# Packing six of eight head groups of an attention block without padding, with a dense output projection for them

## Chip, cores and metric

One NeuronCore of a Trainium2 chip runs the whole program. The metric is the device time of one execution in microseconds (us), of which the median over several runs is used. The kernel before takes 896.84 us (three runs, 896.48 to 897.79).

## What is computed

The input `x` has 2048 rows of 640 columns in bf16. The reference is a transformer block of two parts, with 32 heads of 20 columns each:

```
qkv = layernorm(x) @ wqkv                      # 640 -> 3 x 32 heads x 20
p   = softmax(q @ k.T * 20 ** -0.5)            # per head, 2048 x 2048
h   = x + concat_heads(p @ v) @ wo             # output projection 640 -> 640
l   = layernorm(h)
h2  = h + ((l @ w_gate) * (l @ w_up)) @ w_down # 640 -> 1728 -> 640
```

## The kernel before

**Tiling.** A head of 20 columns is padded to a slot of 32 partitions (`SLOT`), so that four heads (`HPG`) fill the 128 partitions and make a *group*; there are eight groups (`NG`). Queries are taken in four blocks of 512 rows (`QB`, `NB`), and parts of blocks 1 to 3 in halves of 256 (`PASS`, `SPLIT_G`; the passes are named "0", "1", "E", "F", "2", "C", "D", "3", "A", "B"). One pass of one group over all 2048 keys is a *segment*.

**Main loop.** The segments are cut into score tiles of 1536 columns. For each tile the loop emits the score matmuls (`emit_S`, L557), then the exponential on ScalarE from PSUM to a bf16 tile `E` or `El` (L573). For some tiles the last 512 columns are left to VectorE, which computes the exponential with four operations of its own (`emit_x` and its steps: L610, L620, L621, L615). Then the products with the values are accumulated in `acc` (`emit_AV`, L795); an extra row of ones in the values yields the softmax sums. When a segment is complete, VectorE copies `acc` to `asb` (L807).

**Normalisation.** `norm` sends the four rows of sums through DRAM by transfers on SyncE's queue: `sums` out (L666), `sums_all` back in 128 partitions (L667), a reciprocal `ri` on VectorE (L677), `scr` out (L679), and four broadcasts `bc` (L682). A planned number of tiles later `times` multiplies `asb` by `bc` and writes the group's normalised output, a padded 128 x 512 tile `on` (L685). The last group of a half block is not sent through DRAM but normalised on TensorE (`job_norm`: L700, L708, L710, L711, L716, L731), since its result is wanted soonest; the segments so treated are listed in `FAST`. All transfers of the kernel are issued in order on one queue, SyncE's.

**Output projection.** `wo` is held as eight tiles `wo0` to `wo7` of 128 x 640, each with four heads' 20 rows at 32-row steps and zeros between (`load_wo`: eight memsets L987, 32 loads L991). Before that, the first five of these tiles stage a part of `wqkv` at the start of the kernel. `out_mm` computes 128 rows of the output in two halves of 320 columns, each a chain of eight matmuls over the groups (L1052), and VectorE adds `x` (L1056). These jobs, like those of the second layernorm and of the gated part (`glu`, L1221, L1226, L1229) and its last product (`y`, L1270, L1274), are run in pieces in the gaps that the score matmuls leave on TensorE.

**What sets the order.** A planner in the Python code keeps estimates of each engine's time (`at`), the cost of each job and of what is left (`PE_NS`, `ALONE_NS`, used in `room`), and decides from them when a piece of a job runs, when VectorE takes a share of a tile (`x_takes`), and when TensorE gets filler matmuls whose result is not used (`keep_warm`, L508; `cool`, L553). The instruction order of each engine is thus fixed when the program is built, and a changed estimate shifts all that follows.

**The end.** After the last exponential, `last_tail` handles the last 256 rows alone. `out_most` (L1376, L1378) puts `x` and seven of eight groups in PSUM for four half rows, while the last group is normalised on TensorE and VectorE (L700, L708 to L711, L716, L1391); `out_last` (L1382) adds the eighth. Then come the second layernorm (L209 onwards), the gated part (L1203, L1211) and `y`, with nothing of the attention beside them. A general path for inputs whose sums are out of range (`general`) is built as well and not run.

Of the kernel before, what the change touches and what calls it, by code (L numbers as in the profile page):

```python
# [10 lines left out]
BF16 = mybir.dt.bfloat16  # L11
# [5 lines left out]
ALU = mybir.AluOpType  # L17
AX = mybir.AxisListType

P = 128  # L20
S = 2048
D = 640
H = 32
DH = 20
# [3 lines left out]
SLOT = 32  # L28
HPG = 4
NG = H // HPG  # L30
VS = DH + 1
VW = H * VS + (SLOT - VS) + 1
QB = 512
# [5 lines left out]
HALF = D // 2  # L39
FP = 7  # L40
FPW = 256
G1 = 4
SPLIT_G = {"1": 4, "2": 2, "3": 1}
QA = 3 * QB
RES0 = 3
# [24 lines left out]
FULL_IN, FULL_NS, ALL_NS = 2083, 300, 760  # L70
X_LEAST, X_OUT, X_SOON = 2, 5, 4
X_CHUNK = 3
PE_NS = {"out": 6000, "glu": 23000, "y": 7000}
NF_NS = 1800
ALONE_NS = {"out": 4350, "glu": 15260, "y": 5710}
PART_NS, TILE_NS, ROOM = 31500, 700, 2500
E_BUFS, E_LATE = 6, 2
SHIFT = 544.0
# [13 lines left out]
def kernel(  # L92
# [11 lines left out]
    nc = tc.nc  # L104
# [7 lines left out]
    const = pool("const")  # L112
    qkp = pool("qkp")
    vp = pool("vp")
    onp = pool("onp")
# [18 lines left out]
    shift_row = const.tile([P, 1], F32, name="shift_row")  # L134
    huge = const.tile([P, 1], F32, name="huge")
    half = const.tile([P, TPB], F32, name="half")
    wo = [const.tile([P, D], BF16, name=f"wo{g}") for g in range(NG)]
    N_SUMS = 16 * (NB * NG)
    sums_all = const.tile([P, N_SUMS], F32, name="sums_all")

# [2 lines left out]
    qsp = [dram.tile([P, S], BF16, name=f"qsp{g}", bufs=1) for g in range(NG)]  # L143
    kT = [qkp.tile([P, S], BF16, name=f"kT{g}") for g in range(NG)]
    vx = [vp.tile([P, VW], BF16, name=f"vx{t}") for t in range(NT)]
    On = [onp.tile([P, QB], BF16, name=f"on{g}") for g in range(NG)]

    lnT = ra.tile([P, KT, S], BF16, name="lnT")
    wv = [ra.tile([P, D], BF16, name=f"wv{c}") for c in range(KT)]
    wqk = [ep.tile([P, EW], BF16, name="E") for c in range(KT)]  # L150
# [20 lines left out]
        nc.sync.dma_start(xs[0][:, t, :], x2d[t * P:(t + 1) * P, :])  # L171

    def wqk_half(c, hf):
        return (wo if hf else wqk)[c][:, 0:D].rearrange("p (m x) -> p m x", m=2)

    def load_wqk(hf):
        for c in range(KT):
# [170 lines left out]
    for s, (p, g, lo, hi, _) in enumerate(segs):  # L348
        w = PASS[p][2]
        n = BANK // w  # L350
# [305 lines left out]
    def read_out(b):  # L656
        return all(("om", b, t) in done for t in TAILS[b])

    def norm(s, asb):
        p, g = segs[s][0:2]  # L660
        b, c0, w = PASS[p]
        n = w // 32
        r16 = sums_all[:, col["n"]:col["n"] + n]
        col["n"] += n
        sums = dram.tile([HPG, w], F32, name="sums", tag=f"sums{w}")
        nc.sync.dma_start(sums[:], asb[DH:P:SLOT, 0:w])  # L666
        nc.sync.dma_start(r16, sums[:].rearrange("j (c f) -> (j c) f", f=n))  # L667

        due = at["dve"] + SUMS_NS

        def back():
            if at["pe"] < due and now["i"] < n_tiles:
                later(1, back)
                return
            ri = nrm.tile([P, n], F32, name="ri", tag=f"ri{n}")
            dve(130)
            nc.vector.reciprocal(ri[:], r16)  # L677
            scr = dram.tile([HPG, w], F32, name="scr", tag=f"scr{w}")
            nc.sync.dma_start(scr[:].rearrange("j (c f) -> (j c) f", f=n), ri[:])  # L679
            bc = nrm.tile([P, QB], F32, name="bc")  # L680
            for j in range(HPG):
                nc.sync.dma_start(bc[SLOT * j:SLOT * (j + 1), 0:w], scr[j:j + 1, :].to_broadcast([SLOT, w]))  # L682

            def times(asb, bc, p, g, c0, w):
                nc.vector.tensor_tensor(On[g][:, c0:c0 + w], asb[:, 0:w], bc[:, 0:w], ALU.mult)  # L685
                done.add(("n", p, g))
                yield 605 * w // QB

            def mult():
                if b and not read_out(b - 1):  # L690
                    later(1, mult)
                    return
                aux.append(times(asb, bc, p, g, c0, w))
            later(7, mult)
        later(4, back)
# [173 lines left out]
    m32, r = rstd_act(pair_mv[0], 2, lambda: bn(pair_mv[1], 0, xs[0][:, 2, :]))  # L869
# [11 lines left out]
    m32, r = rstd_act(pair_mv[1], 2)  # L881
# [101 lines left out]
                add(("v", t, 1), job_V(t, 1))  # L983

    def load_wo():
        for g in range(NG):
            nc.vector.memset(wo[g][:], 0.0)  # L987
            yield 230
            for j in range(HPG):
                h = HPG * g + j  # L990
                nc.sync.dma_start(wo[g][SLOT * j:SLOT * j + DH, :], A_wo[DH * h:DH * h + DH, :])  # L991
            due = at["pe"] + WO_NS
            while at["pe"] < due and not now["forced"]:
                yield WAIT

    def make_identf():
        nc.vector.tensor_copy(identf[:], ident[:])
# [49 lines left out]
    def out_mm(on, st, t):  # L1047
        for hf in range(2):
            ps = bank()
            cs = slice(hf * HALF, (hf + 1) * HALF)  # L1050
            for g in range(NG):
                nc.tensor.matmul(ps[:, 0:HALF], lhsT=on[g][:, t * P:(t + 1) * P], rhs=wo[g][:, cs],  # L1052
                                 start=(g == 0), stop=(g == NG - 1))
                if g == NG - 1:
                    dve(408, 136)
                    nc.vector.tensor_tensor(st["h"][t][:, cs], ps[:, 0:HALF], st["xr"][t][:, cs], ALU.add)  # L1056
                yield 136
            done.add(("oh", t, hf))
            yield NEXT
# [306 lines left out]
    def last_tail():  # L1366
        st = tail_st[LAST_B]
        on = On
        asb = final["asb"]
        c0 = LAST_T[0] * P  # L1370
        ps_h = {}

        def out_most(t, hf):
            ps = ps_h[t, hf] = bank()
            cs = slice(hf * HALF, (hf + 1) * HALF)
            nc.tensor.matmul(ps[:, 0:HALF], lhsT=ident[:], rhs=st["xr"][t][:, cs], start=True, stop=False)  # L1376
            for g in range(NG - 1):
                nc.tensor.matmul(ps[:, 0:HALF], lhsT=on[g][:, t * P:(t + 1) * P], rhs=wo[g][:, cs], start=False, stop=False)  # L1378

        def out_last(t):  # L1380
            for hf in range(2):
                nc.tensor.matmul(ps_h[t, hf][:, 0:HALF], lhsT=on[NG - 1][:, t * P:(t + 1) * P],  # L1382
                                 rhs=wo[NG - 1][:, hf * HALF:(hf + 1) * HALF], start=False, stop=True)
        ta, tb = LAST_T
        out_most(ta, 0)
        bc = sums_to_rows(sums_on_pe(asb, HW), HW)
        out_most(ta, 1)
        ps = rows_to_cols(bc, HW, accp.tile([P, QB], F32, name="acc"))
        for k in range(2):
            cs = slice(k * P, (k + 1) * P)  # L1390
            nc.vector.tensor_tensor(on[NG - 1][:, c0 + k * P:c0 + (k + 1) * P], asb[:, cs], ps[:, cs], ALU.mult)  # L1391
        out_most(tb, 0)
        out_last(ta)
        out_most(tb, 1)
        out_last(tb)
        mv = small.tile([P, 2, 2], F32, name="mv")
        for k, t in enumerate(LAST_T):
            bn(mv, k, None, [ps_h[t, hf][:, 0:HALF] for hf in range(2)])
        m32, r = rstd_act(mv, 2)
        mr = small.tile([P, 2], F32, name="mr")  # L1400
        nc.vector.scalar_tensor_tensor(mr[:], m32[:], -1.0, r[:], ALU.mult, ALU.mult)
        ls = {t: late["s"].tile([P, D], BF16, name="ln2") for t in LAST_T}
        for hf in range(2):
            cs = slice(hf * HALF, (hf + 1) * HALF)
            nc.vector.tensor_scalar(ls[ta][:, cs], ps_h[ta, hf][:, 0:HALF], m32[:, 0:1], r[:, 0:1], ALU.subtract, ALU.mult)
            nc.scalar.activation(ls[tb][:, cs], ps_h[tb, hf][:, 0:HALF], ACT.Identity, bias=mr[:, 1:2], scale=r[:, 1:2])
        begun = at["pe"]
        while at["pe"] - begun < LN_NS and step() is not None:
            pass
        idle_n = int((LN_NS - (at["pe"] - begun)) / 216)  # L1410
        if idle_n > 0:
            warm_ps = bank()
            for _ in range(idle_n):
                nc.tensor.matmul(warm_ps[:], lhsT=ident[:], rhs=kT[0][:, 0:BANK], start=True, stop=True)
        run(job_T(ls[ta], st["ln2T"][:, :, ta * P:(ta + 1) * P], "dve", mip.tile([P, D], BF16, name="mi", tag="mi")))
        run(job_T(ls[tb], st["ln2T"][:, :, tb * P:(tb + 1) * P], "act", accp.tile([P, QB], F32, name="acc")[:].bitcast(BF16)[:, 0:D]))
        fill()
        for t in LAST_T:
            for hf in range(2):
                nc.scalar.copy(st["h"][t][:, hf * HALF:(hf + 1) * HALF], ps_h[t, hf][:, 0:HALF])  # L1420
        st["w", 2] = [w_tile(src, 2, ep.tile([P, EW], BF16, name="E")) for src in (B_w_up, B_w_gate)]
        n_next = 0
        for c in job_glu(st, LAST_T, tuple(range(RES0, FP)) + tuple(range(RES0))):
            n_next += c == NEXT
            if c == NEXT and n_next == 8:
                ok = flag_ok()
            if c == NEXT and n_next == 20:
                flag_bad(ok)
        run(job_y(st, LAST_T, True))
# [85 lines left out]
    def general():  # L1515
        st = new_st(None)
        st["res"] = {}
        with tc.For_i(0, S, P) as r0:
# [3 lines left out]
            for g in range(NG):  # L1522
# [39 lines left out]
                nc.vector.tensor_tensor(oq[:, :, 0:DH], ov[:, :, 0:DH], ri[:].to_broadcast([P, HPG, DH]), ALU.mult)  # L1562
                ps = bank(BF16, P)
                nc.tensor.transpose(ps[:], oq[:].rearrange("p j e -> p (j e)"), ident[:])
                nc.vector.tensor_copy(On[g][:, 0:P], ps[:])
            for fn in (job_out(On, st, [0], None), job_glu(st, [0]), job_y(st, [0])):
                for _ in fn:
                    pass
# [33 lines left out]
```

## Time and profile before

| | |
|---|---|
| median of three runs | 896.84 us |
| the profiled execution | 900.67 us |
| its span in the profile | 898.8 us |
| ScalarE (ACT) busy | 852.7 us, 95% |
| TensorE (PE) busy | 813.7 us, 91% |
| VectorE (DVE) busy | 773.7 us, 86% |
| all transfers | 60.15 MB, a mean of 67 GB/s |

In the profile PE is TensorE's matmuls, PEld its weight loads, DVE VectorE, ACT ScalarE, POOL GpSimd, and SPq the queue of SyncE, on which the transfers are issued. A row of a timeline gives the start in us, the time to the end of the last of the instructions merged in it, the engine, the line, the operation, and `out<-in`; in brackets is the idle time of the engine ahead of it and what ended that. A row of waits gives the total in us, the number of times, and the longest. Windows give busy us and the number of instructions of each engine in a stretch, then the clock that TensorE was granted (1.00 is full), the share of the transfer engines and GB/s.

### The profile page before, as it was taken

The page shows a single profiled execution, that of the slowest core. Times are in us where ns is not written, and L with a number is a line of the kernel's source. Part 1 is how long each engine was busy: PE and PEld are TensorE (multiplying, and loading weights), DVE is VectorE, ACT ScalarE, POOL GpSimd, SP SyncE. Part 2 cuts the span into 40 slices and gives each one's busy share as a digit, 9 for nine tenths or more (in the row PEclk, how much of TensorE's full clock was granted, in tenths as well). Part 3 has the DMA queues.
Part 4 walks back from the last instruction along what each step waited for, and adds up shares of the span by engine and source line. Part 5 has one row for each costly group of instructions (what it writes and reads, how often), then busy time and mean ns, then how long its engine had stood idle before and what let it go on. Part 6 is the DMA issues. An engine that isn't in the chain of part 4 may idle for free.

```text
span 898.8 us, 21965 instructions
## 1 busy us (share of the span) xinstructions
PE 813.7 (91%) x8921; PEld 374.1 (42%) x8921; DVE 773.7 (86%) x1448; ACT 852.7 (95%) x719; POOL 31.4 (3%) x122
## 2 busy tenths in 40 slices
PE   7889999989999899889999998998899999999997
PEld 5333232222233344544444554443434455444465
DVE  7778899999999899789999998999889988889842
ACT  6999999999999999989999999999999999999951
POOL 4100000000002000001000000001000000000000
PEclk9999999999999999989999999999989999999999
DMA  6030010011034556432214334111441312010310
GB/s 198 25 65 2 1 28 25 15 36 28 14 84 112 122 146 198 112 88 66 54 51 122 81 96 107 47 30 29 121 121 45 85 31 74 15 44 9 94 38 18
DMA packets 110763, 60.15 MB, mean 67 GB/s; under 512 B 37976, under 2 KB 107652, under 8 KB 110656
## 3 DMA queue, kind: packets, MB, share of 16 engines
q1 hardware_dynamic: 110656, 58.68, 25.0%
q8 instruction: 72, 1.18, 0.6%
q14 instruction: 35, 0.29, 0.1%
HBM read 48.09 MB, written 7.28 MB: 62 GB/s over the span
## 4 chain that ended last, share of the span: by engine, by line
ACT 56%; PE 21%; issue 13%; DVE 9%; DMA 1%; SPq 0%; ACTq 0%; DVEq 0%
ACT E L573 46%; ACT El L573 10%; PE sc L557 5%; PE mi L1221 3%; PE acc L795 3%; PE f L1203 2%; PE mi L306 1%; PE mi L1052 1%; DVE xv L610 1%; PE mi L1270 1%; PE f L1270 1%; DVE xt L620 1%; DVE xt L621 1%; DVE xe L615 1%; DVE hh L1229 1%
## 5 line engine op out<-in xcount | busy, mean ns | idle before, releaser
L573 ACT ACTIVATE E<-sc 128x1536 bf16<-128x1536 f32 (+1 forms) x560 | 694.0, 1387 | 7.3 <-PE sc L557 6.0
L557 PE MATMUL sc<-qa,kT 32*128 32x256 bf16 (+1 forms) x2176 | 204.1, 320 | 23.8 <-ACT E L573 13.5
L557 PEld LDWEIGHTS <-kT 32*128 32x128 bf16 x3136 | 85.2, 92 | 223.9 <-issue 193.4
L610 DVE TENSOR_SCALAR xv<-sc 128x512 f32<-128x512 f32 x199 | 137.1, 690 | 47.3 <-PE sc L557 44.4
L573 ACT ACTIVATE El<-sc 128x1536 bf16<-128x1536 f32 (+1 forms) x123 | 159.7, 1371 | 0.6 <-PE sc L557 0.5
L795 PE MATMUL acc<-E,vx 128*32 128x256 bf16 (+1 forms) x2245 | 158.2, 315 | 0.6 <-DVE vx L271 0.6
L615 DVE SCALAR_TENSOR_TENSOR xe<-xt,xv 128x512 int16<-128x512 f32 x199 | 134.3, 681 | 0.8
L621 DVE SCALAR_TENSOR_TENSOR xt<-xt,xv 128x512 f32<-128x512 f32 x199 | 133.2, 680 | 0.6
L620 DVE SCALAR_TENSOR_TENSOR xt<-xv 128x512 f32<-128x512 uint16 x199 | 132.1, 679 | 0.3 <-DVE ri L677 0.2
L306 PE MATMUL mi<-lnT,wp 128*128 128x512 bf16 x305 | 86.5, 381 | 7.1 <-DVE qa L313 3.4
L795 PEld LDWEIGHTS <-vx 128*32 128x32 bf16 x3136 | 62.2, 96 | 62.5 <-issue 60.6
L557 PE MATMUL sc<-qb,kT 32*128 32x256 bf16 (+1 forms) x960 | 69.0, 283 | 3.4 <-ACT E L573 2.2
L1270 PE MATMUL mi<-wd,hh 128*128 128x320 bf16 x378 | 65.5, 301 | 1.1 <-DVE xr L1274 1.0
L1221 PE MATMUL mi<-ln2T,wg 128*128 128x256 bf16 x390 | 56.7, 274 | 8.6 <-DVE u L1226 7.2
L1221 PE MATMUL mi<-ln2T,wu 128*128 128x256 bf16 x390 | 55.5, 274 | 7.4 <-DVE hh L1229 7.2
L795 PE MATMUL acc<-El,vx 128*32 128x256 bf16 (+1 forms) x579 | 60.6, 294 | 0.5 <-ACT El L573 0.5
L795 PE MATMUL acc<-xe,vx 128*32 128x256 bf16 (+1 forms) x312 | 57.3, 306 | 0.0
L1270 PEld LDWEIGHTS <-hh 128*128 128x128 bf16 x448 | 37.9, 97 | 29.5 <-issue 18.2
L1221 PEld LDWEIGHTS <-wg 128*128 128x128 bf16 x390 | 33.6, 97 | 30.0 <-issue 25.3
L306 PEld LDWEIGHTS <-wp 128*128 128x128 bf16 x310 | 24.8, 97 | 50.6 <-issue 38.5
L1221 PEld LDWEIGHTS <-wu 128*128 128x128 bf16 x390 | 33.8, 97 | 28.3 <-issue 25.1
L1052 PE MATMUL mi<-wo,on 128*128 128x320 bf16 x224 | 41.6, 312 | 2.3 <-DVE xr L1056 2.2
(152 smaller groups left out, 623.0 us busy)
## 6 DMA issues: line engine op xcount, KB each, us to landing
wu<-in_B_w_up_dram SPq DMA_DIRECT2D x38, 320.0 KB
wg<-in_B_w_gate_dram SPq DMA_DIRECT2D x37, 320.0 KB
bc<-scr SPq DMA_DIRECT2D x60, 64.0 KB
bc<-scr SPq DMA_DIRECT2D x108, 32.0 KB
qsp<-qa SPq DMA_DIRECT2D x8, 384.0 KB
xr<-in_A_x_dram SPq DMA_DIRECT2D x16, 160.0 KB
out_dram<-xr SPq DMA_DIRECT2D x14, 160.0 KB
wd<-in_B_w_down_dram SPq DMA_DIRECT2D x13, 160.0 KB
```

The costliest lines, as they stand in the source:

```text
L306: nc.tensor.matmul(ps[:], lhsT=wslice(m, g, c), rhs=lnT[:, c, ch * QB:(ch + 1) * QB], start=(c == 0), stop=(c == KT - 1))
L557: nc.tensor.matmul(sc[:, o:o + w], lhsT=kT[g][SLOT * j:SLOT * (j + 1), kt * P:(kt + 1) * P], rhs=q_of(g, b, c0, w)[SLOT * j:SLOT * (j + 1) ...
L573: exps = nc.scalar.activation(e[:, 0:n_act], sc[:, 0:n_act], ACT.Exp, bias=EXP_BIAS, scale=SM_SCALE)
L610: took = nc.vector.tensor_scalar(v[:], ps, X_SCALE, X_BASE, ALU.mult, ALU.max)
L615: nc.vector.scalar_tensor_tensor(e[:], t[:], X_R, v[:], ALU.mult, ALU.add)
L620: lambda: nc.vector.scalar_tensor_tensor(t[:], u, X_P, u, ALU.add, ALU.mult),
L621: lambda: nc.vector.scalar_tensor_tensor(t[:], t[:], X_Q, u, ALU.add, ALU.mult),
L795: nc.tensor.matmul(acc["t"][SLOT * j:SLOT * (j + 1), 0:w], lhsT=vx[kt][:, VS * h:VS * h + SLOT], rhs=e, start=(acc["n"][j] == 0), stop=(ac ...
L1052: nc.tensor.matmul(ps[:, 0:HALF], lhsT=on[g][:, t * P:(t + 1) * P], rhs=wo[g][:, cs], start=(g == 0), stop=(g == NG - 1))
L1203: nc.tensor.matmul(ps[:, 0:n], lhsT=st["w", fp][k][:, c, f_cols(fp, f2)], rhs=st["ln2T"][:, c, c0:c0 + n], start=(c == 0), stop=(c == KT - 1))
L1221: nc.tensor.matmul(ps[:, f2 * n:(f2 + 1) * n], lhsT=st["w", fp][k][:, c, f_cols(fp, f2)], rhs=st["ln2T"][:, c, c0:c0 + n], start=(c == 0), ...
L1270: nc.tensor.matmul(ps[:, 0:HALF], lhsT=st["hh"][f // 2][:, f % 2, t * P % HW:t * P % HW + P], rhs=late["Wd"][f][:, cs], start=(f == 0), st ...
```

## The change

The outputs of groups 0 to 5 (24 heads, 480 rows) are kept without padding in four tiles `d0` to `d3` of 128, 128, 128 and 96 rows; groups 6 and 7 stay padded. The multiplication of `norm` writes a padded tile `on` from a pool of two for groups 0 to 5, and `pack` copies each head's 20 rows from there to their place, SBUF to SBUF, by one transfer on SyncE's queue (two where a head crosses a tile's border). The weights of `wo` for these groups are loaded as four dense tiles. Each chain of the output projection has six matmuls in place of eight. The planner's costs of an output job are set lower. In `last_tail`, the last group's matmul goes through the same helper.

```
-PE_NS = {"out": 6000, "glu": 23000, "y": 7000}
+PE_NS = {"out": 4900, "glu": 23000, "y": 7000}
-ALONE_NS = {"out": 4350, "glu": 15260, "y": 5710}
+ALONE_NS = {"out": 3264, "glu": 15260, "y": 5710}
...
+PADDED = (6, 7)
+DENSE = ("d0", "d1", "d2", "d3")
+OUT_ROWS = {"d3": 96}
...
-    wo = [const.tile([P, D], BF16, name=f"wo{g}") for g in range(NG)]
+    wo = {k: const.tile([P, D], BF16, name=f"wo{k}") for k in DENSE + PADDED}
-    On = [onp.tile([P, QB], BF16, name=f"on{g}") for g in range(NG)]
+    On = {k: onp.tile([P, QB], BF16, name=f"on{k}") for k in DENSE + PADDED}
...
+    def pack(o, g, cols):
+        for j in range(HPG):
+            r, d = DH * (HPG * g + j), 0
+            while d < DH:
+                n = min(DH - d, P - (r + d) % P)
+                to = (r + d) % P
+                nc.sync.dma_start(On[DENSE[(r + d) // P]][to:to + n, cols], o[SLOT * j + d:SLOT * j + d + n, cols])
+                d += n
...
             def times(asb, bc, p, g, c0, w):
-                nc.vector.tensor_tensor(On[g][:, c0:c0 + w], asb[:, 0:w], bc[:, 0:w], ALU.mult)
+                cols = slice(c0, c0 + w)
+                o = On[g] if g in PADDED else onp.tile([P, QB], BF16, name="on", bufs=2)
+                nc.vector.tensor_tensor(o[:, cols], asb[:, 0:w], bc[:, 0:w], ALU.mult)
+                if g not in PADDED:
+                    pack(o, g, cols)
...
     def load_wo():
-        for g in range(NG):
+        for k, key in enumerate(DENSE):
+            n = OUT_ROWS.get(key, P)
+            nc.sync.dma_start(wo[key][0:n, :], A_wo[P * k:P * k + n, :])
+        for g in PADDED:
             nc.vector.memset(wo[g][:], 0.0)
...
+    def out_product(ps, key, t, cs, start, stop):
+        n = OUT_ROWS.get(key, P)
+        nc.tensor.matmul(ps[:, 0:HALF], lhsT=On[key][0:n, t * P:(t + 1) * P], rhs=wo[key][0:n, cs], start=start, stop=stop)
...
-            for g in range(NG):
-                nc.tensor.matmul(ps[:, 0:HALF], lhsT=on[g][:, t * P:(t + 1) * P], rhs=wo[g][:, cs],
-                                 start=(g == 0), stop=(g == NG - 1))
-                if g == NG - 1:
+            for key in DENSE + PADDED:
+                out_product(ps, key, t, cs, key == DENSE[0], key == PADDED[-1])
+                if key == PADDED[-1]:
...
-            for g in range(NG - 1):
-                nc.tensor.matmul(ps[:, 0:HALF], lhsT=on[g][:, t * P:(t + 1) * P], rhs=wo[g][:, cs], start=False, stop=False)
+            for key in (DENSE + PADDED)[:-1]:
+                out_product(ps, key, t, cs, False, False)
```

The general path gets the same packing, and the staging of `wqkv` uses the first five of the six weight tiles that are left.

More of the change, by code (lines that the diff above doesn't have):

```diff
@@ L173, in wqk_half @@
     def wqk_half(c, hf):
-        return (wo if hf else wqk)[c][:, 0:D].rearrange("p (m x) -> p m x", m=2)
+        return (list(wo.values()) if hf else wqk)[c][:, 0:D].rearrange("p (m x) -> p m x", m=2)
     def load_wqk(hf):
@@ L1376, in out_most @@
             nc.tensor.matmul(ps[:, 0:HALF], lhsT=ident[:], rhs=st["xr"][t][:, cs], start=True, stop=False)
-            for g in range(NG - 1):
-                nc.tensor.matmul(ps[:, 0:HALF], lhsT=on[g][:, t * P:(t + 1) * P], rhs=wo[g][:, cs], start=False, stop=False)
+            for key in (DENSE + PADDED)[:-1]:
+                out_product(ps, key, t, cs, False, False)
         def out_last(t):
             for hf in range(2):
-                nc.tensor.matmul(ps_h[t, hf][:, 0:HALF], lhsT=on[NG - 1][:, t * P:(t + 1) * P],
-                                 rhs=wo[NG - 1][:, hf * HALF:(hf + 1) * HALF], start=False, stop=True)
+                out_product(ps_h[t, hf], NG - 1, t, slice(hf * HALF, (hf + 1) * HALF), False, True)
         ta, tb = LAST_T
@@ L1564, in general @@
                 nc.tensor.transpose(ps[:], oq[:].rearrange("p j e -> p (j e)"), ident[:])
-                nc.vector.tensor_copy(On[g][:, 0:P], ps[:])
+                o_t = On[g] if g in PADDED else onp.tile([P, QB], BF16, name="on", bufs=2)
+                nc.vector.tensor_copy(o_t[:, 0:P], ps[:])
+                if g not in PADDED:
+                    pack(o_t, g, slice(0, P))
             for fn in (job_out(On, st, [0], None), job_glu(st, [0]), job_y(st, [0])):
```

## The prediction

> **What bounds the kernel now.** I read the page first, for the busy shares and the chain that ended last, and then two windows, before and after the last exponential at 858.8 us.
>
> ```profile
> span 898.8 us, 21965 instructions
> ACT 56%; PE 21%; issue 13%; DVE 9%; DMA 1%; SPq 0%; ACTq 0%; DVEq 0%
> ```
>
> ```profile
> 60.00:858.00 798.00, 730.54 (x8227) 324.42 (x8228) 711.08 (x1279) 791.89 (x652) 16.52 (x39) 0.99 0.26 67
> 858.00:899.00 41.00, 33.77 (x287) 26.12 (x279) 16.06 (x48) 10.70 (x25) 0.00 (x0) 0.96 0.11 31
> ```
>
> The columns are TensorE, its weight loads, VectorE and ScalarE. Between 60 and 858 us ScalarE is busy for 791.89 of 798 us: the exponentials bound this stretch, and everything else can win at most the 6.1 us in which ScalarE stood still. In the last 41 us it is a chain of TensorE and VectorE that counts. So I ask of each edit: does it take columns from ScalarE, does it touch the 6.1 us, or does it lie in the last chain?
>
> Who took the 6.1 us? The waits of ScalarE name scores that came late:
>
> ```profile
> ACT E L573 <- PE sc L557: 4.3, 6, 2.0
> ACT El L573 <- PE sc L557: 0.5, 2, 0.3
> ```
>
> The two largest pieces lie where an output job has just begun, and there TensorE's clock is down (0.66 and 0.67, the third column from the end):
>
> ```profile
> 395.00:405.00 10.00, 9.26 (x101) 4.54 (x100) 7.08 (x15) 7.68 (x7) 0.00 (x0) 0.66 0.01 2
> 650.00:660.00 10.00, 9.01 (x52) 3.38 (x53) 7.67 (x16) 8.56 (x8) 0.00 (x0) 0.67 1.14 304
> ```
>
> ```profile
> 401.40 2.05 PE L1052 MATMUL mi<-wo,on 128*128 128x320 bf16 x7
> ...
> 404.12 4.63 ACT L573 ACTIVATE E<-sc 128x1024 bf16<-128x1024 f32 x4 [2.05 <-PE sc L557]
> ```
>
> Seven output matmuls took 2.05 us at 401.40, and the exponential at 404.12 waited 2.05 us for scores queued behind them. Both places come just after a group is normalised on TensorE, where there is no other job to run; the clock falls in that pause.
>
> **The change part by part.**
>
> *Matmuls of the output projection.* 32 chains (16 row tiles, two halves) lose two matmuls each. Four of them are in the last tail, so 56 of the 64 lie in the loop. There a matmul costs about 0.135 us (in the tail row below, 7 in 1.11 us with 0.30 for the last), so 7.6 us of TensorE. The changed kernel's instruction list has 20 more filler matmuls of L508 and 3 fewer of L553: the planner sees idle time and fills it. At about 0.22 us each 3.7 us come back, and TensorE loses some 4 us of 730. ScalarE hides this, and I count 0. Its bounds: -4.8 us, if all of ScalarE's waits for scores vanish; and above, see the clock below.
>
> *The last tail* is on the path, and there I go step by step.
>
> ```profile
> 858.81 0.29 PE L795 MATMUL acc<-El,vx 128*32 128x256 bf16 x2 [0.50 <-ACT El L573]
> ...
> 859.24 0.42 DVE L807 COPY asb<-acc 128x256 f32<-128x256 f32 x1 [5.98 <-PE acc L795]
> 859.28 1.11 PE L1378 MATMUL f<-wo,on 128*128 128x320 bf16 x7
> ...
> 860.23 0.50 PE L700 MATMUL f<-identf,asb 128*128 128x4 f32 x4
> ...
> 860.83 0.21 DVE L708 RECIPROCAL ri<-f 128x8 f32<-128x8 f32 x1 [1.17 <-PE f L700]
> ...
> 861.28 0.16 DVE L711 COPY sums_all<-f 128x8 f32<-128x8 f32 x1
> ...
> 861.68 0.61 PE L716 MATMUL acc<-identf,bc 128*128 128x128 f32 x4
> 862.12 0.30 PE L1376 MATMUL f<-xr,ident 128*128 128x320 bf16 x1
> ...
> 862.33 0.48 DVE L1391 TENSOR_TENSOR on<-asb,acc 128x128 bf16<-128x128 f32 x2 [0.89 <-PE acc L716]
> 863.21 0.43 PE L1382 MATMUL f<-wo,on 128*128 128x320 bf16 x2
> ...
> 863.55 0.90 DVE L209 BATCH_NORM_STATS2 st<-f 128x6 f32<-128x320 f32 x2 [0.74 <-PE f L1382]
> ...
> 864.57 0.43 PE L1382 MATMUL f<-wo,on 128*128 128x320 bf16 x2
> 864.91 0.89 DVE L209 BATCH_NORM_STATS2 st<-f 128x6 f32<-128x320 f32 x2 [0.22 <-PE f L1382]
> ```
>
> Here is the latency from VectorE to TensorE for this very pair of lines:
>
> ```profile
> 851.81 0.16 DVE L711 COPY sums_all<-mi 128x8 f32<-128x8 f32 x1
> 852.12 0.68 PE L716 MATMUL mi<-identf,bc 128*128 128x128 f32 x4 [0.23 <-DVE sums_all L711]
> ```
>
> L711 ends at 851.97 and L716 starts at 852.12: 0.15 us. Now the tail with six matmuls in each block in place of eight. L700 waits for its turn on TensorE (`asb` is ready at 859.66), so it starts 2 x 0.135 = 0.27 us sooner, at 859.96, and L708 to L711 with it; L711 ends at 861.17. The second block leaves TensorE free at 861.14, but L716 has to wait for 861.17 + 0.15 = 861.32: 0.36 us sooner, not 0.54. L1391 then ends at 862.45, and L1382 can start at 862.60 (the third block is done at 862.57): 0.61 us sooner. The first statistics move by as much and their last, small step ends at 864.08 (before at 864.69). The fourth block lets the second L1382 start at 863.68, so the second statistics no longer wait for TensorE but for VectorE itself, at about 864.12 against 864.91. **The tail is worth -0.80 us.** From there the chain runs on VectorE, and TensorE's filler ahead of the transposes moves by as much.
>
> *Columns of ScalarE.* The changed list has 200 tiles shared with VectorE where the trace has 199; one exponential is 1024 wide in place of 1536.
>
> ```profile
> 845.15 1.94 ACT L573 ACTIVATE E<-sc 128x1024 bf16<-128x1024 f32 x2 [0.23 <-ACT E L573]
> ...
> 849.64 8.20 ACT L573 ACTIVATE E<-sc 128x1536 bf16<-128x1536 f32 x6
> ```
>
> 8.20 / 6 - 1.94 / 2 = 0.40 us less. In the list, the last values products are put off: 14 of them stand behind the wait for the last exponential where 6 did. They run four at a time, a round each 0.10 us (rows at 858.81 and 858.91), so the last copy comes 0.2 to 0.3 us later: +0.25. **Together -0.15 us.**
>
> *Packing.* 158 transfers are added to SyncE's queue in the executed part (27, 36, 45 and 50 for the four blocks), and 32 loads of `wo` become 12.
>
> ```profile
> L682 SPq DMA_DIRECT2D bc<-scr x168: 302/414/1632, 121.7 to 847.3; - x168
> ```
>
> ```profile
> L991 SPq DMA_DIRECT2D wo<-in_A_wo_dram x32: 281/328/338, 187.6 to 215.9; - x32
> ```
>
> 158 x 0.414 - 20 x 0.328 = 59 us of issuing, over some 720 us. That queue mostly waits for others:
>
> ```profile
> SPq L666 <- DVE asb L807: 118.3, 27, 17.5
> ```
>
> So it has room on the whole, but a pack stands as a lump of four or five (1.7 to 2.1 us) in front of the next group's `sums`, `scr`, `bc` or weights, and each transfer behind it is that much later. No transfer SBUF to SBUF stands in the trace; its landing I bound by `sums`, 1.6 us from issue to the next step that needs it (807.81 to 809.43), and by `scr` in a crowded place, 4.4 us (371.04 to 375.40):
>
> ```profile
> 807.81 0.50 SPq L666 DMA_DIRECT2D sums<-asb  x1
> 809.43 0.34 SPq L667 DMA_DIRECT2D sums_all<-sums  x1
> ```
>
> ```profile
> 371.04 0.55 SPq L679 DMA_DIRECT2D scr<-ri  x1
> 375.40 1.79 SPq L682 DMA_DIRECT2D bc<-scr  x4
> ...
> 379.62 0.43 DVE L685 TENSOR_TENSOR on<-asb,bc 128x256 bf16<-128x256 f32 x1 [0.33 <-DMA bc<-scr]
> ```
>
> Who waits for packs? First, the output job: but its last two matmuls read the padded groups 6 and 7, which are normalised last, some 7 us and more behind group 5. Tightest is the last tail: group 5's multiplication was at 851.9 and stays just ahead of group 6's; nine transfers (groups 4 and 5) take 3.7 us and land by 857.2 to 860.0, and the first dense matmuls come at 859.3. I take 0, the nearer end, with +0.7 above. Second, VectorE, whose third multiplication needs the first's tile back: they are mostly over 10 us apart, so 0. Third, all that is behind them on the queue; I take 0, since a usual group has 4 us and more between landing and use, with +6 above (below, rival C). Six memsets of 0.325 us go from VectorE, against one more shared tile: 0 either way.
>
> The Trainium skill, page "DMA: Bandwidth & Descriptors", section "Rules for kernel authors", speaks against the change: many small transfers should be coalesced, since under 64 KB one pays mostly overhead. The trace agrees as far as it goes: a 4 KB `sums` takes 1.6 us, issue included. By that rule each pack would be all overhead; whether this costs time hangs on who waits, which is rival C.
>
> **Sum.** -0.80 - 0.40 + 0.25 = -0.95 us against the span of 898.8, so 897.85. The profiled execution took 900.67 us, 1.87 around its span, and lies above the median of 896.84; I take the difference over to the median: **895.9 us**, 0.11% less.
>
> **The rivals.**
>
> A, *faster: the scores no longer wait.* The output jobs at 401 and 657 us are where ScalarE waited; two matmuls less at the head of each, or a clock that does not fall there, could give back most of 4.3 + 0.5 us. For: in the changed list the pause before the output job at the second place is three tiles, not six. Against: at the first it is as long as before, and filler comes in. Half of 4.8 and the sum give 895.9 - 2.4 = 893.5 us.
>
> B, *slower: the clock falls more often.* Freed TensorE time is idle time unless filler comes in time. One fall as at 395 to 405 us cost ScalarE 10 - 7.68 = 2.3 us; two more give 895.9 + 4.6 = 900.5, and it decides from the second. For: in the list, the third normalisation on TensorE is followed by six tiles with hardly any full matmul. Against: the planner's filler grew by 20.
>
> The Trainium skill, "TensorE: Matmul & The Clock Gate", section "Part 1: The HAM clock gate", says that the clock halves after an idle window of about 3.4 us. The trace shows falls to 0.66 as a mean of 10 us in such pauses, so it agrees in kind; B is what that rule would do here.
>
> C, *slower: the packs hold up SyncE's queue.* Place: 350 to 400 us, where weights and spills crowd it. The multiplication at 379.62 already waited 0.33 us, so there is no slack left: from a delay of `bc` by over 0.3 us, VectorE stands, then the single spare bank, TensorE, and after about one exponential of 1.37 us ScalarE. Three multiplications there, each up to 2.1 us later: between 3 x 0.7 and 3 x 2.1 us, so 898.0 to 902.2; I put it at 900. Against: elsewhere such waits sum to nothing in the trace.
>
> D, *the change gives nothing:* TensorE's time goes to filler, the tail is eaten by late packs (+0.7): 896.6, within the forecast's own range.
>
> **How the numbers follow.** Forecast, with D: 0.45 (895.1 to 898.6). A: 0.27. B: 0.14. C: 0.14. Differences under 0.2%, 1.8 us, can't be told from no change. So faster 0.27, same 0.45, slower 0.28. The range leaves out the far half of C and B and the best third of A: 893.0 to 900.5.
>
> **What would show it.** The tail: L700 some 0.27 us sooner behind the last `asb`, L209 the second time with no wait for TensorE. ScalarE busy some 0.4 us less. For A, ScalarE's waits for scores under 3 us in all; for B, more windows with a clock under 0.9; for C, VectorE waiting for `bc` by more than 0.3 us, or TensorE for weights. Wrong would be the whole if ScalarE's idle time between 60 and 858 us changed by over 2 us, since I hold it equal.

## The result, and the profile after

The changed kernel takes **926.42 us** (median of six runs, 922.63 to 928.87) against 896.66 us (six runs, 894.95 to 898.69) of the kernel before on the same chip: 1.0326 times, with a 95% interval of 1.0300 to 1.0352. It is slower by 30 us where 1 us less was forecast. The profiled execution took 924.72 us, 1.82 around its span; before it was 1.87, so the difference lies within the span. (The two spans differ by 24.1 us and the medians by 30, since the profiled execution of the kernel before is 4 us above its median and this one 1.7 us below.) The page's lines for the span and for the chain that ended last:

```profile
span 922.9 us, 22050 instructions
...
ACT 43%; PE 24%; issue 13%; DVE 11%; DMA 6%; SPq 2%; DVEq 0%; ACTq 0%
```

ScalarE has lost 13 points of the chain. Transfers hold 6% of it where they held 1%, and SyncE's queue 2% where it held none: somebody now waits for data. The windows up to the end of the last exponential (881.5 us) and after it, with TensorE, its weight loads, VectorE, ScalarE and GpSimd, then the clock:

```profile
60.00:881.50 821.50, 725.68 (x8129) 322.02 (x8179) 711.93 (x1275) 793.64 (x652) 18.05 (x39) 0.98 0.26 68
881.50:923.00 41.50, 32.71 (x275) 25.48 (x275) 16.01 (x48) 9.99 (x25) 0.00 (x0) 0.94 0.11 30
```

ScalarE does the same work (793.64 us, before 791.89 up to 858 us and 0.76 more to its last exponential at 858.76), but stands still for 821.5 - 793.64 = 27.9 us instead of 6.1. Of the 24.1 us by which the span grew, 21.7 are this idle time. The waits say what it is made of (total, times, longest):

```profile
ACT E L576 <- PE sc L560: 22.4, 20, 3.5
...
DVE ri L689 <- DMA sums_all<-sums: 7.8, 4, 3.7
...
PEld L1243 <- DMA wg<-in_B_w_gate_dram: 6.6, 5, 2.5
...
ACT El L576 <- PE sc L560: 6.0, 3, 2.9
...
PE mi L1243 <- DMA ln2T<-ln: 4.5, 2, 2.5
...
PEld L1243 <- DMA wu<-in_B_w_up_dram: 3.7, 4, 1.6
DVE on L699 <- DMA bc<-scr: 3.6, 2, 2.6
DVE ln L247 <- DMA ln2T<-ln: 3.6, 2, 2.8
```

ScalarE waits for scores, 28.4 us in all (6.5 us before). What TensorE and VectorE wait for gives the reasons: `sums_all`, the weights `wg` and `wu`, the transposed `ln2T`, `bc`. None of these transfers was touched by the change. What they share is SyncE's queue, and there the packs are. This is the row of the pack's line (shortest, median and longest issue in ns):

```profile
L668 SPq DMA_DIRECT2D ond<-on x158: 554/714/1592, 135.5 to 877.9; - x158
```

0.714 us each, 113 us together; four or five packs fill the queue for 3 to 4 us. Five places hold 22 of the 27.9 us:

```profile
290.00:310.00 20.00, 15.01 (x110) 6.19 (x109) 14.03 (x26) 15.45 (x14) 0.83 (x2) 0.83 0.50 125
390.00:400.00 10.00, 6.45 (x66) 3.27 (x66) 7.07 (x13) 5.91 (x5) 0.00 (x0) 0.83 0.46 120
440.00:450.00 10.00, 6.78 (x85) 3.08 (x85) 7.92 (x14) 7.33 (x8) 0.00 (x0) 0.87 0.41 70
650.00:670.00 20.00, 15.46 (x173) 6.99 (x162) 11.45 (x21) 13.65 (x11) 0.00 (x0) 0.74 0.39 104
860.00:870.00 10.00, 6.23 (x53) 1.79 (x48) 4.38 (x9) 5.61 (x5) 0.00 (x0) 0.69 0.23 60
```

ScalarE's missing time is 4.6, 4.1, 2.7, 6.4 and 4.4 us, and in each of them the granted clock is down too. Not all of it is owed to the packs: for the fifth place see experiment 1. The second place, read in the timeline from the packs to the exponential:

```profile
379.10 3.58 SPq L668 DMA_DIRECT2D ond<-on  x5
...
382.78 0.52 SPq L691 DMA_DIRECT2D scr<-ri  x1
...
386.14 1.73 SPq L694 DMA_DIRECT2D bc<-scr  x4
...
387.97 0.54 SPq L678 DMA_DIRECT2D sums<-asb  x1
...
389.68 0.35 SPq L679 DMA_DIRECT2D sums_all<-sums  x1
...
391.29 0.20 DVE L689 RECIPROCAL ri<-sums_all 128x8 f32<-128x8 f32 x1 [3.51 <-DMA sums_all<-sums]
...
392.70 0.61 PE L560 MATMUL sc<-qa,kT 32*128 32x256 bf16 x6 [2.74 <-DVE xv L613]
...
393.44 1.45 ACT L576 ACTIVATE E<-sc 128x1536 bf16<-128x1536 f32 x1 [2.23 <-PE sc L560]
```

Five packs take the queue until 382.68. Behind them, each after the other, come one group's `scr`, its `bc`, and the next group's `sums` and `sums_all`. VectorE reaches the reciprocal that wants `sums_all` 3.51 us too soon and stands; behind that reciprocal in its order is the freeing of a score bank (`xv`), so TensorE stands 2.74 us, and ScalarE 2.23 us. At the first place it is the transposes for the second layernorm:

```profile
289.62 3.08 SPq L668 DMA_DIRECT2D ond<-on  x4
...
293.34 3.44 SPq L1171 DMA_TRANSPOSE ln2T<-ln  x2
...
298.23 2.10 PE L1243 MATMUL mi<-ln2T,wu 128*128 128x256 bf16 x9 [2.46 <-DMA ln2T<-ln]
```

The end behaves as forecast:

```profile
882.22 0.42 DVE L823 COPY asb<-acc 128x256 f32<-128x256 f32 x1 [2.44 <-PE acc L811]
...
882.94 0.50 PE L716 MATMUL f<-identf,asb 128*128 128x4 f32 x4
...
884.22 0.68 PE L732 MATMUL acc<-identf,bc 128*128 128x128 f32 x4
...
885.90 0.90 DVE L212 BATCH_NORM_STATS2 st<-f 128x6 f32<-128x320 f32 x2 [0.47 <-PE f L1017]
...
886.99 0.90 DVE L212 BATCH_NORM_STATS2 st<-f 128x6 f32<-128x320 f32 x2
```

From the copy to the second statistics it takes 4.77 us (before 5.67), and that statistics waits for nothing.

### The profile page after: what moved, and what is told of

It reads as the page before. It is cut to its first block, busy times and chain, and to the rows that moved or that the text cites. A ratio compares the mean times of both kernels' runs of the same rounds, so it can differ in the third digit from the quotient of the medians.

```text
span 922.9 us, 22050 instructions
## 1 busy us (share of the span) xinstructions
PE 809.2 (88%) x8817; PEld 372.3 (40%) x8874; DVE 774.5 (84%) x1446; ACT 854.4 (93%) x719; POOL 33.0 (4%) x122
## 4 chain that ended last, share of the span: by engine, by line
ACT 43%; PE 24%; issue 13%; DVE 11%; DMA 6%; SPq 2%; DVEq 0%; ACTq 0%
ACT E L576 36%; ACT El L576 7%; PE mi L1243 6%; PE sc L560 6%; PE acc L811 4%; DVE xv L613 2%; PE f L1225 2%; PE mi L1292 2%; DMA scr<-ri 2%; DVE xt L623 1%; DVE xt L624 1%; DVE hh L1251 1%; PE mi L309 1%; SPq L694 1%; PE f L1292 1%
## 5 line engine op out<-in xcount | busy, mean ns | idle before, releaser
L576 ACT ACTIVATE E<-sc 128x1536 bf16<-128x1536 f32 (+1 forms) x561 | 694.9, 1379 | 23.3 <-PE sc L560 22.4
L309 PE MATMUL mi<-lnT,wp 128*128 128x512 bf16 x280 | 82.6, 381 | 8.7 <-DVE qa L316 3.4
L1243 PE MATMUL mi<-ln2T,wu 128*128 128x256 bf16 x410 | 61.9, 283 | 14.0 <-DVE hh L1251 7.9
L1243 PE MATMUL mi<-ln2T,wg 128*128 128x256 bf16 x410 | 62.2, 282 | 13.5 <-DVE u L1248 10.4
L811 PE MATMUL acc<-xe,vx 128*32 128x256 bf16 (+1 forms) x315 | 60.3, 311 | 0.3 <-issue 0.3
L1243 PEld LDWEIGHTS <-wg 128*128 128x128 bf16 x410 | 36.1, 100 | 38.5 <-issue 27.8
L1243 PEld LDWEIGHTS <-wu 128*128 128x128 bf16 x410 | 36.5, 100 | 37.4 <-issue 26.8
L511 PE MATMUL mi<-kT,ident 128*128 128x512 bf16 x101 | 34.8, 402 | 8.7 <-DVE xr L1296 4.7
```

What stands on the lines that cost most here:

```text
L309: nc.tensor.matmul(ps[:], lhsT=wslice(m, g, c), rhs=lnT[:, c, ch * QB:(ch + 1) * QB], start=(c == 0), stop=(c == KT - 1))
L511: nc.tensor.matmul(ps[:], lhsT=ident[:], rhs=kT[0][:, 0:BANK], start=True, stop=True)
L576: exps = nc.scalar.activation(e[:, 0:n_act], sc[:, 0:n_act], ACT.Exp, bias=EXP_BIAS, scale=SM_SCALE)
L811: nc.tensor.matmul(acc["t"][SLOT * j:SLOT * (j + 1), 0:w], lhsT=vx[kt][:, VS * h:VS * h + SLOT], rhs=e, start=(acc["n"][j] == 0), stop=(ac ...
L1243: nc.tensor.matmul(ps[:, f2 * n:(f2 + 1) * n], lhsT=st["w", fp][k][:, c, f_cols(fp, f2)], rhs=st["ln2T"][:, c, c0:c0 + n], start=(c == 0), ...
```

## The experiments

Each kernel was timed beside the kernel before on the same chip; ratios are to that kernel, which took 896.3 to 896.8 us in each group of runs.

**1. Without the packs.** The multiplication still writes the padded tile.

```
-                if g not in PADDED:
-                    pack(o, g, cols)
...
+            nc.gpsimd.memset(On[key][:], 0.0)
```

> The changed kernel without the 158 packs: the dense tiles are set to zero once and hold zeros, so groups 0 to 5 add nothing to the output projection; all matmuls, waits for the padded groups, and the planner's costs are those of the changed kernel. Theory Q (the packs' issues, 158 of 0.71 us in lumps of 3 to 4 us, stand in front of other transfers on SyncE's queue): back to 895 to 897 us, ScalarE's waits for scores under 6 us, and the tail still 0.8 us shorter. Theory T (the packs' transfers load the 16 DMA engines): the same, so this run doesn't part Q from T. Theory P (fewer matmuls and other planner costs move the order of the work and let the clock fall more often): still above 915 us.

897.43 us, 1.0016 (0.9991 to 1.0041). ScalarE's waits for scores, 22.4 us in the changed kernel, are near what the kernel before had (6.0 us), a little over theory Q's 6:

```profile
ACT E L576 <- PE sc L560: 6.5, 9, 1.6
...
839.93 0.20 DVE L689 RECIPROCAL ri<-sums_all 128x8 f32<-128x8 f32 x1 [2.87 <-DMA sums_all<-sums]
```

The time is 0.4 us above Q's range, and from the copy `asb` to the second statistics it takes 4.77 us, as in the changed kernel. Without the packs no loss is left that can be measured, and P falls: in sum, the changed order and the shorter chains cost nothing by themselves. They bring nothing either; the forecast's 0.11% less is just outside this interval. But the order has moved a wait. The reciprocal at 839.93 us is the one that stands 3.71 us at the fifth place of the changed kernel; here, without any pack, it waits 2.87 us for the `sums_all` of a `sums` that was issued just behind four loads of weights, and ScalarE stands still for 2.8 us between 840 and 850 us. By this comparison the packs made the smaller part of the fifth place's 4.4 us.

**2. The packs alone, in the kernel before.**

```
                 nc.vector.tensor_tensor(On[g][:, c0:c0 + w], asb[:, 0:w], bc[:, 0:w], ALU.mult)
+                if g < 6:
+                    pack(On[g], g, slice(c0, c0 + w))
```

> The kernel before with the packs added: after each multiplication of groups 0 to 5 the same 158 transfers go, on SyncE's queue, from the padded tile into one spare tile that nothing reads; output projection and planner stay padded. Theories Q and T: 918 to 930 us, VectorE waiting for sums_all, bc and ln2T by 10 us and more. Theory P: 896 to 899 us.

914.05 us, 1.0210 (1.0159 to 1.0260): 18 us from transfers whose result nobody reads, 4 us short of the range. The same waits come up in its trace as in the changed kernel:

```profile
ACT E L574 <- PE sc L558: 15.3, 17, 2.5
...
DVE ri L687 <- DMA sums_all<-sums: 7.2, 6, 2.3
...
DVE on L695 <- DMA bc<-scr: 5.9, 5, 2.0
...
PEld L1233 <- DMA wu<-in_B_w_up_dram: 5.4, 4, 2.9
```

**3. The packs on another queue.** Three kernels have the packs issued by GpSimd: the changed kernel; the kernel before, to a spare tile; and the changed kernel, to a spare tile.

```
-                nc.sync.dma_start(On[DENSE[(r + d) // P]][to:to + n, cols], o[...])
+                nc.gpsimd.dma_start(On[DENSE[(r + d) // P]][to:to + n, cols], o[...])
```

> The changed kernel with the 158 packs issued by GpSimd's queue in place of SyncE's. Theory Q: 893 to 900 us, ScalarE's waits for scores back under 6 us; the transfers are the same, so theory T: still above 915 us. Theory P: still above 915 us.

902.57 us, 1.0075 (1.0045 to 1.0105). 24 of the 30 us are gone; 6 stay, 2.6 us above Q's range. ScalarE's waits for scores missed Q's 6 us as well: 13.1 us in the profiled execution, the slowest of the eight (907.8 us).

> The kernel before with the 158 packs added, issued by GpSimd's queue, into one spare tile that nothing reads: the transfers without SyncE's queue, without the dense projection and without any wait for them. If the 6 us that stayed with the packs on GpSimd's queue are the load of the transfers on the DMA engines (theory T, as the smaller part): 901 to 905 us. If they are the waits of the dense projection, or the order of its work: 895 to 898 us.

896.06 us, 1.0016 (0.9991 to 1.0042). The second line of the expectation.

> The changed kernel with its packs issued by GpSimd's queue and written to one spare tile that nothing reads (the dense tiles hold zeros, so groups 0 to 5 add nothing to the output projection). It parts the 6 us that the packs on GpSimd's queue still cost. If it is the waits between packs and output matmuls: 895 to 898 us. If it is the order of the changed kernel's work, which bears late transfers worse: 901 to 904 us.

898.07 us, 1.0017 (0.9993 to 1.0041), a touch above its first line. The transfers' load on the DMA engines thus costs nothing that can be measured here, in the old order or in the new: T falls. What counts is that the packs were issued on SyncE's queue. Moving them off it could also help by letting the other small transfers land sooner once they are issued. The times that SyncE waits for `scr` and `sums` to land, in the kernel before and in the changed one, speak against that:

```profile
SPq L682 <- DMA scr<-ri: 66.4, 42, 3.8
SPq L667 <- DMA sums<-asb: 47.9, 38, 2.3
...
SPq L694 <- DMA scr<-ri: 62.2, 42, 3.8
SPq L679 <- DMA sums<-asb: 53.8, 38, 3.8
```

They sum to 114 us before and 116 us after: for these it is the turn on the queue that comes late, not the landing. How soon the weights land, these rows don't show.

The Trainium skill, "DMA: Bandwidth & Descriptors", section "Issuing engines are not separate DMA queues", says that issuing from several engines saves only the sequencer's time to start a transfer, usually small beside the transfer itself. The runs agree with the first half. As to the second, a pack takes 0.714 us to issue on SyncE and, where it was measured, on GpSimd's queue, 2.3 us (median) to land; yet taking these issues off SyncE's queue was worth 24 us of 926, since others' transfers stood behind them.

Of the 6 us that stayed, some 4.5 are, by the pair of 902.57 and 898.07, the waits between packs and output matmuls; no single row that carries them was found. That the matmuls read zeros in the second of the two does not explain it: in experiment 6 zeros in the padded projection left the time as it was (914.01 against 914.05 us).

**4. What on the queue costs: waiting, lumps, or the sum of issue time?** In the changed kernel SyncE also stands in front of packs, waiting for VectorE's work:

```profile
SPq L668 <- DVE on L699: 27.1, 5, 8.6
...
SPq L668 <- DVE xv L613: 7.5, 6, 2.7
```

First the lump was put off (with four buffers for the padded tile):

```
+                    def go(o=o):
+                        pack(o, g, cols)
+                        done.add(("n", p, g))
+                    later(5, go)
```

> The changed kernel with each group's packs (a lump of 4 or 5, on SyncE's queue as before) put off by 5 tiles, some 7 us, after the multiplication, with four buffers for the padded tile. SyncE then finds the multiplication done and has not to wait for it. Theory Q1 (what costs is the time in which SyncE stands still in front of a pack, waiting for the multiplication: 46 us in all in the changed kernel): under 908 us. Theory Q2 (what costs is the issue time of the lumps, 3 to 4 us each): 915 to 930 us, since the lumps are as long as before and stand elsewhere.

923.88 us, 1.0305 (1.0274 to 1.0335). The wait for the multiplication shrank, and the time by 2.5 us, with intervals that overlap:

```profile
SPq L668 <- DVE on L699: 3.9, 3, 2.3
```

Q1 falls. Then one pack at a time, one per tile (`later(1, one)` for each):

> The changed kernel with the packs put off by 5 tiles and then issued singly, one each tile of 1.4 us, on SyncE's queue, four buffers for the padded tile. No lump is left, the sum of issue time is the same. Theory Q2 (the lumps): 896 to 906 us, below the run with lumps put off. Theory Q1: the same as that run, within 3 us. If the sum of issue time counts and not the lumps: above 915 us.

915.65 us, 1.0219 (1.0185 to 1.0253). Both of the first two theories missed; the third line, "above 915 us", just held. But the trace shows that the edit did not do what was expected of it:

```profile
447.26 4.46 SPq L673 DMA_DIRECT2D ond<-on  x6
...
PEld L1256 <- DMA wg<-in_B_w_gate_dram: 8.8, 8, 2.5
...
PEld L1256 <- DMA wu<-in_B_w_up_dram: 6.5, 4, 3.3
PE mi L1256 <- DMA wg<-in_B_w_gate_dram: 6.4, 3, 2.2
PE mi L1256 <- DMA wu<-in_B_w_up_dram: 5.5, 3, 3.0
```

The program puts one pack after each tile, but SyncE, held up elsewhere, still issues packs back to back: 17 of the 158 stand alone, and 71 are in runs of four and more. So breaking the lumps up in part is worth about 8 us against the run before, 19 us stay, and whether those are the lumps that are left or the sum of the issue time this run doesn't tell. What the packs now delay is the weights: TensorE waits 27 us in all for them, where it waited 14.7 in the changed kernel.

**5. Which transfers behind the packs matter?** The weights alone were moved off the queue.

```
-        nc.sync.dma_start(view[:, :, 0:w], src[...])
+        nc.gpsimd.dma_start(view[:, :, 0:w], src[...])
```

> The changed kernel with the loads of the two weights of the gated unit issued by GpSimd's queue in place of SyncE's, the packs left on SyncE's. In the changed kernel TensorE waits 14.7 us in all for these weights, VectorE 13 us for sums_all, bc and the padded tile, and both together 11 us for ln2T. If the weights' lateness is the larger part of the loss: under 912 us. If the chain of the sums and ln2T carry it: 916 to 928 us. A rival to both: the loads wait on GpSimd's queue for a free buffer and hold up the small steps of the second normalisation there: above 930 us.

919.35 us, 1.0238 (1.0194 to 1.0281). TensorE waits for weights no longer, but

```profile
ACT E L576 <- PE sc L560: 22.5, 19, 5.0
...
DVE ri L689 <- DMA sums_all<-sums: 6.6, 2, 6.2
...
PE mi L1243 <- DMA ln2T<-ln: 4.9, 2, 3.1
...
DVE ln L247 <- DMA ln2T<-ln: 4.1, 2, 3.7
```

the chain of the sums and `ln2T` keep ScalarE's waits nearly where they were: 26.2 us in all with those of `El`, against 28.4. Some 7 us came back, out of 14.7 us of waits removed, which fits the second line: the waits cover for one another.

**6. Why 30 us and not 18?** The packs alone cost 18 us, in the changed kernel 30. First, two buffers against four for the padded tile (`name="on", bufs=4`):

> The changed kernel with four buffers in place of two for the padded tile that the multiplication writes and the packs read. Theory W (VectorE waits for a pack to land before it may write the tile again): under 910 us, and the wait of 1.7 us for that tile gone. Theory Q: 920 to 930 us, since the queue is as full as before.

926.46 us, 1.0347 (1.0308 to 1.0386): the wait for the tile is gone from the trace, the time is the same, and W falls. Then the changed kernel with its packs to a spare tile:

> The changed kernel with its packs, at their place in SyncE's queue, written to one spare tile that nothing reads; the dense tiles hold zeros, so groups 0 to 5 add nothing to the output projection. What it leaves out of the changed kernel is only that a pack waits for the output matmuls of the block before, and that output matmuls wait for packs. If these waits make the 12 us by which the changed kernel is slower than the kernel before with packs added: about 914 us. If the order of the work or the longer lumps make them: 922 to 930 us.

921.70 us, 1.0277 (1.0244 to 1.0309), 0.3 us below the second line. The waits between packs and matmuls are worth some 4.7 us here, much as with GpSimd's queue, though the interval and that of the changed kernel overlap a little; about 7 us are neither. Are they the planner's costs?

> The changed kernel with the planner's costs of an output job as they were (6000 and 4350 in place of 4900 and 3264); packs, dense projection and SyncE's queue as changed. If the planner's order makes the part of the 30 us that packs alone (18 us) do not: 910 to 917 us. If not: 921 to 930 us.

925.08 us, 1.0322 (1.0285 to 1.0359).

> The kernel before with the packs added on SyncE's queue into one spare tile, and with the planner's costs of the changed kernel (4900 and 3264). If the planner's order makes the rest: 920 to 930 us. If not: 911 to 918 us, as with the packs alone.

913.70 us, 1.0192 (1.0154 to 1.0230). No, in both directions. The shared tile that the multiplication writes, or the six matmuls in place of eight?

```
+                o = On[g] if g >= 6 else onp.tile([P, QB], BF16, name="or", bufs=2)
```

> The kernel before with the packs added on SyncE's queue into one spare tile, and with the multiplications of groups 0 to 5 written to the two shared tiles of the changed kernel; the output projection keeps its eight padded matmuls and reads zeros for groups 0 to 5. If the shared tiles make the 7 us between the packs alone (914) and the packs in the changed order (921.7): 919 to 925 us. If the six matmuls make them: 911 to 918 us.

914.01 us, 1.0188 (1.0158 to 1.0219). Not the tile; nor do the zeros that the matmuls read here change the time.

```
-            for g in range(NG):
+            for g in (0, 1, 2, 3, 6, 7):
```

> The kernel before with the packs added on SyncE's queue into one spare tile, and with groups 4 and 5 left out of the output projection, so that a chain has six matmuls as in the changed kernel. If the six matmuls make the 7 us: 919 to 925 us. If the shared tiles make them: 911 to 918 us.

917.58 us, 1.0233 (1.0206 to 1.0259): within its second line (911 to 918), by which six matmuls don't make the 7 us. Still, it is 3.5 us above the packs alone, with intervals that overlap, so they may make a part; the rest stays open. The same order without packs on SyncE's queue costs nothing (897.43 and 898.07 us in experiments 1 and 3), so the rest shows only together with late data; how is not shown.

## Why the prediction was wrong, point by point

**What bounds the kernel: right.** ScalarE's work changed by 1 us, its idle time by 21.7 us, and idle time of ScalarE was what the text said to look for.

**The tail: right.** Forecast -0.80 us from the copy `asb` on, measured 4.77 against 5.67: -0.90, each step within about 0.1 us of the working (L716 0.72 us after the copy where L700 came 0.99 after it). The last values products came 0.20 us later (copy 0.68 us after the last exponential, before 0.48), for +0.25. Tail packs cost nothing. The rest of the end grew by 2.0 us, all of it between the issue of the last outputs and the span's end (12.9 us, before 10.9). In the experiments that start from the kernel before this took 10.0 to 11.3 us, in those that start from the changed one 11.0 to 13.4; what makes the difference was not sought.

**Columns of ScalarE: not seen.** -0.40 us was forecast; ScalarE was busy 1.0 us more. This is small, and its cause was not sought.

**Matmuls of the output projection: right.** TensorE lost 4.9 us up to the last exponential (730.54 to 725.68), where some 4 were forecast. It was counted at nothing; experiment 1 measures nothing.

**Packing is the step that failed.** It was counted at 0, because "a usual group has 4 us and more between landing and use", with +6 us as the upper end. Two things in it were wrong. The issue was priced by the broadcasts' 0.414 us; a pack takes 0.714 us, so that a lump of four or five takes 3.0 to 4.6 us and not "1.7 to 2.1". And the slack was taken per transfer. But a group's way through DRAM is a chain of `sums`, `sums_all`, `scr` and `bc` on one queue; a lump that meets it is paid there once and again for the transfers of the next group, of the layernorm and of the weights behind it. The 4 us were not there: at the second place one lump of 3.58 us, passed on from `scr` to the next group's `sums_all`, left VectorE waiting 3.51 us. The bound of +6 us was the bound of rival C's one place, not of the queue.

**Rival C was the mechanism**, with the steps that it named: `bc` or its like late, VectorE, the bank, TensorE, ScalarE. The signs that it named came: VectorE waited 3.6 us for `bc`, and TensorE 14.7 us for weights. Its place (350 to 400 us) was one of five. That its price fits there is in part luck: 2.1 to 6.3 us were reckoned for three late multiplications, and ScalarE lost 4.1 us between 390 and 400, but by one reciprocal late for `sums_all`; and the 2.3 us that the kernel before lost just behind, between 400 and 410 us, are gone. What spoke against it, that "elsewhere such waits sum to nothing in the trace", was true of the kernel before and no bound for the changed one.

**Rival A happened at its two places, and brought nothing.** In experiment 1, ScalarE stands still for 0.0 us between 400 and 410 and between 650 and 660 us, where the kernel before lost 2.3 and 1.4; 2.8 us came up at 840 to 850 us in their place.

**Rival B happened, but as a consequence.** Freed TensorE time did not lower the clock: of the stretches of 10 us from 60 us to the end of the loop, three have a clock under 0.9 in the kernel before, three in experiment 1 and eight in the changed kernel. The clock fell where TensorE stood for late data, to 0.69 to 0.87 in the windows above, and slowed what had to be caught up. That the falls made the loss larger is argued from these rows; no run parts the two.

**Who waits for packs: partly wrong.** VectorE's wait for its tile back was counted at 0; it came once, for 1.7 us, and taking it away changed nothing (experiment 6). The waits between packs and output matmuls were counted at 0, with +0.7 us above, and cost about 4.5 us.

**The Trainium skill's warning** that small transfers are mostly overhead (same page, "Rules for kernel authors") was weighed and left to rival C. The trace agrees as to the issue: a pack of 10 or 20 KB takes 0.714 us on SyncE's queue, a load of `wg`, mostly 320 KB, 0.470 (medians). That one larger transfer per group costs less was not tried.

## What to carry to other kernels

Before transfers are added to a queue, list everything that the queue carries behind them, and ask of each chain of dependent transfers how often it meets the new ones; slack of one transfer is not slack of the chain. Price the issue of a new kind of transfer with a margin (here 0.714 us against 0.414 of the nearest row, a factor of 1.7), or issue it from a queue on which nothing urgent stands. Moving it off the queue is also the quickest experiment: it tells the cost of the queue from that of the data.

## What the hardware showed that was not expected

The same transfer has different issue times on different queues. These are the packs to the spare tile in the kernel before, on SyncE's queue (experiment 2) and on GpSimd's (experiment 3):

```profile
L666 SPq DMA_DIRECT2D od<-on x158: 554/712/1420, 136.0 to 869.0; - x158
...
L666 POOL DMA_DIRECT2D od<-on x158: 505/509/755, 132.4 to 849.4; - x158
```

On SyncE's queue the median is 0.712 us, though a broadcast of more bytes takes 0.413 there; on GpSimd's it is 0.509. And 158 of them on GpSimd's queue, 80 us of GpSimd's time, with nothing waiting behind them, left the time where it was (896.06 us).
